# Split weights laid 2,080 bytes apart, at eight places modulo 64 bytes, in a three-block fp32 kernel

## The chip, the cores and the metric

The kernel runs on one core of one Trainium2 chip. The metric is the device time of one execution in microseconds. Before the change two runs took 833.51 and 834.58 us, median 834.05 us.

## What is computed

Three blocks follow each other on 4 sequences of 576 tokens with 512 features (2,304 tokens, 18 tiles of 128): a windowed attention with 8 heads, a block that mixes tokens and then features, and a feature block behind a normalization. Cut to what matters:

```python
def _moe_ref(x, w_tok1, w_tok2, w_ch1, w_ch2):
    h = np.maximum(x.transpose(0, 2, 1) @ w_tok1, 0.0) @ w_tok2
    u = x + h.transpose(0, 2, 1)
    return u + np.maximum(u @ w_ch1, 0.0) @ w_ch2          # 512 -> 1536 -> 512

def _moe2_ref(x, g_ln, w_ch1, w_ch2):
    mu, var = np.mean(x, -1, keepdims=True), np.var(x, -1, keepdims=True)
    xn = (x - mu) / np.sqrt(var + 1e-06) * g_ln
    return x + np.maximum(xn @ w_ch1, 0.0) @ w_ch2         # 512 -> 2048 -> 512

x = _attn_ref(q, k, v)        # window 128, a slope of distance for each head
return _moe2_ref(_moe_ref(x, ...), ...)
```

## The kernel before

**Split products.** A float32 product is made of three TensorE products. Each operand is split into a high part in float32r and a low part that holds the rest: a = ah + al, and a·b is taken as ah·bh + ah·bl + al·bh. Each product is one MATMUL, with a weight load (LDWEIGHTS) of its own for the operand that stands in the array. The other operand moves: 512 or 256 columns of 4 bytes are read from SBUF for each MATMUL.

**The two feature blocks.** They are walked in steps (list `steps`): a layer has three stages, of 8, 2 and 8 tiles of tokens, and each stage goes through all inner features, 12 blocks of 128 in layer 0 and 16 in layer 1. A step takes two blocks.

- `seven_products` (L1109) makes the first product of a wide step by Strassen-like sums: seven products of 6 MATMULs (L1125 to L1127). Here a split weight (w1h, w1l) stands in the array, 128 columns at a time, and a split input (x..., names xh and xl in the profile) moves, 512 columns.
- `two_blocks` (L1210) does a step of two tiles through `mm3` (L469 to L471): w1 stands, the inputs (fewh, fewl) move, 256 columns.
- `second` (L1223) makes the second product: inner features (hh, hl) stand, split weights (w2h, w2l) move, 512 columns (L1238 to L1240).
- `second_fast` (L1248) does the second product of one stage of layer 1 by seven products of 256 columns (L1275). There the moving weights are w2h and w2l in some products, and sums of weights in the buffers rw, rh and y in the others.

The first product of a step and the second product of the step before it are interleaved, six MATMULs of one by three to six of the other.

**Where the split weights come from.** `w_split` (L945) takes two buffers for each weight from the pool mlq: ACT copies the high part (L384), POOL or DVE subtracts the low part (L402, L400). `w2_of` (L1024) splits w2 only in the first stage of a layer; it stores both parts to DRAM, and in the later stages it loads them again into buffers of the same ring with two DMAs of 256 KB (L1038). The rings: w1h, w1l, w2h and w2l have four buffers each (W1_BUFS, W2_BUFS).

**Where buffers lie.** A `Buf` becomes a tile of a pool when it is first used (L101), and the tile framework lays a tag's buffers one behind another. A [128, 512] float32 buffer has 2,048 bytes in each partition. In the built program the pools stand so that each of the 16 split-weight buffers, each input buffer (pools mlp and mlr, and few in the pool hid) and each inner-feature buffer (hid) begins 32 bytes past a multiple of 64. The buffers rw, rh and y (pools raw and cvt) begin at a multiple of 64. The pool `even` (L359, 256 columns) takes up what lies between, so that mlp and mlr join without a gap. It is filled once with zeros by POOL (L777).

**What sets the order.** A list scheduler (`Plan.order`) gives every operation a place on its engine from fixed costs; addresses play no part in it. PE takes its MATMULs in that order.

Of the kernel before, what the change touches and what calls it, by code (L numbers as in the profile page):

```python
# [11 lines left out]
F32R = mybir.dt.float32r  # L12
# [12 lines left out]
P = 128  # L25
DM = H * D
# [8 lines left out]
CW = CT * P  # L35
HW = CW // 2
W_BUFS = 6
EVEN = 256
X_BUFS, TOK_RATE = 3, 3
Q_BUFS = 3  # L40
T_BUFS, PF_BUFS = 4, 4
W1_BUFS, W2_BUFS, ST_BUFS, H_BUFS = 4, 4, 6, 6
# [49 lines left out]
class Buf:  # L92


    def __init__(self, plan, pool, shape, dtype, tag, bufs):
        self.plan, self.pool, self.spec = plan, pool, (shape, dtype, tag, bufs)
        self.tile, self.ops, self.track = None, [], {}
        self.after, self.behind, self.first = [], None, set()

    @property  # L100
    def t(self):  # L101
        if self.tile is None:
            shape, dtype, tag, bufs = self.spec
            self.tile = self.plan.pools[self.pool].tile(shape, dtype, tag=tag, name=tag, bufs=bufs)
        return self.tile


class Part(Buf):


# [10 lines left out]
class Plan:  # L121
# [19 lines left out]

        self.chain = {}

    def buf(self, pool, shape, dtype, tag, bufs=1):
        b = Buf(self, pool, shape, dtype, tag, bufs)
        ring = self.rings.setdefault((pool, tag), [])
        if len(ring) >= bufs:
            b.after = [ring[-bufs]]
        if ring:
            b.behind = ring[-1]  # L150
        ring.append(b)
        return b
# [184 lines left out]
def block_kernel(tc, qT, kT, v, wt1, wt2, wa1, wa2, wb1, wb2, g, bias, out):  # L337
# [3 lines left out]
    buf = pl.buf  # L341

    def op(cost, emit, reads=(), writes=(), behind=()):
        return pl.op(cost, (lambda e: emit()) if len(cost) == 1 else emit, reads, writes, behind)
# [16 lines left out]


    even = buf("even", [P, EVEN], F32, "even")
    ident = buf("const", [P, P], F32, "ident")
    g_sb = buf("const", [P, DM // P, 1], F32, "g_sb")
    mv = buf("const", [P, NTILE, 2], F32, "mv")
    rstd = buf("const", [P, NTILE], F32, "rstd")
# [38 lines left out]
    def split(hi, ghi, lo, glo, x, gx, n, on_hi=("ACT", "DVE", "POOL"), on_lo=("DVE", "POOL")):  # L406
        copy(hi, ghi, x, gx, n, on_hi)
        minus(lo, glo, x, gx, hi, lambda: ghi().bitcast(F32), n, on_lo)
# [127 lines left out]
    def take_w():  # L536
        used[0] += 1
        return wtiles[used[0] - 1]
# [404 lines left out]
        return out  # L943

    def w_split(tag, bufs, x, get=None, n=DM, to=None):  # L945
        hi, lo = to or (buf("mlq", [P, DM], F32R, tag + p, bufs) for p in "hl")
        get = get or (lambda: x.t)
        split(hi, lambda: hi.t[:, :n], lo, lambda: lo.t[:, :n], x, get, n, ("ACT",))
        return hi, lo
# [12 lines left out]
    def w1_of(s, ahead=None):  # L962

        f1, f2 = take_w(), take_w()
        if len(steps[s][2]) == 2:
            out = [w_split("w1", W1_BUFS, x) for x in (f1, f2)]
            keep_taken(2)
            return out
# [23 lines left out]
        def parts(early=lambda: None):  # L992
            w0 = w_split("w1", W1_BUFS, f1, to=early())
            if ahead != "few":
                sums_a()
            w1 = w_split("w1", W1_BUFS, a, all_of(a), to=early())
            if ahead != "few":
                sums_b()
            return w0, w1
# [18 lines left out]
    parts2, sums2 = {}, {}  # L1018

    def fast2(s):  # L1020
        layer, c, _, n = steps[s]
        return (layer, c) in FAST2 and n < (NF1, NF2)[layer] // 2 - 1

    def w2_of(s):  # L1024
        out = []
        layer, c, _, n = steps[s]
        last = [mark[0]]
        for f in (2 * n, 2 * n + 1):
            if c == 0:
                x = w_split("w2", W2_BUFS, take_w())  # L1030
                for p, y in zip("hl", x):
                    d = parts2[layer, f, p] = buf("dram", [P, DM], F32, f"d2{layer}{f}{p}")
                    op({"DMA": 728}, lambda d=d, y=y: nc.sync.dma_start(out=d.t, in_=y.t.bitcast(F32)), [y], [d], last)
            else:
                x = []
                for p in "hl":
                    y, d = buf("mlq", [P, DM], F32R, "w2" + p, W2_BUFS), parts2[layer, f, p]
                    op({"DMA": 728}, lambda d=d, y=y: nc.sync.dma_start(out=y.t.bitcast(F32), in_=d.t), [d], [y])  # L1038
                    x.append(y)
            out.append(x)  # L1040
        if c == 0 and (layer, 2) in FAST2 and n < (NF1, NF2)[layer] // 2 - 1:
            keep_sums(layer, n, wtiles[used[0] - 2:used[0]], last)
        return sums_of(layer, n, out) if fast2(s) else out

    def keep_sums(layer, n, w, last):

        x0, x1 = w
        places = few()
        d = {p: buf("dram", [P, 2 * DM], F32, f"ds{layer}{n}{p}") for p in "hl"}

        def all_of(k):
            return places[0], lambda: places[0].t.bitcast(F32)[:, k, :DM]

        def part(c):
            return (places[0], c // 2), lambda: places[0].t.bitcast(F32)[:, c // 2, c % 2 * HW:(c % 2 + 1) * HW]

        def half(x, c):
            return x, lambda: x.t[:, c * HW:(c + 1) * HW]

        def sub(c, a, b):  # L1060
            (x, k), get = part(c)
            minus((x, c), get, *a, *b, HW, ("POOL",))

        def at(c):
            return (places[0], c), part(c)[1]

        sub(0, half(x0, 1), half(x0, 0))
        sub(1, half(x1, 1), at(0))
        sub(2, half(x0, 1), half(x1, 1))
        sub(3, half(x1, 0), at(1))  # L1070
        for k in range(2):
            f, h = [(places[0], 2 * k), (places[0], 2 * k + 1)], (places[1], k)

            def gf(k=k):
                return places[0].t[:, k, :DM]

            def gh(k=k):
                return places[1].t[:, k, :DM]

            copy(h, gh, f, lambda gf=gf: gf().bitcast(F32), DM, ("ACT",))  # L1080
            minus(f, gf, f, lambda gf=gf: gf().bitcast(F32), h, lambda gh=gh: gh().bitcast(F32), DM, ("POOL",))
            for p, z, gz in (("h", [h], gh), ("l", f, gf)):
                op({"DMA": 728}, lambda k=k, p=p, gz=gz: nc.sync.dma_start(
                    out=d[p].t[:, k * DM:(k + 1) * DM], in_=gz().bitcast(F32)), z, [(d[p], k)], last)
        sums2[layer, n] = d

    def sums_of(layer, n, parts):

        d = sums2[layer, n]
        hi = buf("raw", [P, 2 * DM], F32R, "rw", 2)  # L1090
        hs = [((hi, None), lambda k=k: hi.t[:, k * HW:(k + 1) * HW]) for k in range(4)]
        if n % 2:
            lo = [buf("cvt", [P, DM], F32R, "y", 2) for _ in range(2)]
            ls = [((lo[k // 2], None), lambda k=k: lo[k // 2].t[:, k % 2 * HW:(k % 2 + 1) * HW]) for k in range(4)]
        else:
            lo = [buf("raw", [P, 2 * DM], F32R, "rh", 1)]
            ls = [((lo[0], None), lambda k=k: lo[0].t[:, k * HW:(k + 1) * HW]) for k in range(4)]
        for p, xs in (("h", [hi]), ("l", lo)):
            w = 2 * DM // len(xs)
            for k, x in enumerate(xs):  # L1100
                op({"DMA": 1456 / len(xs)}, lambda p=p, k=k, x=x, w=w: nc.sync.dma_start(
                    out=x.t.bitcast(F32), in_=d[p].t[:, k * w:(k + 1) * w]), [d[p]], [x])
        w = {f"t{k + 1}": (hs[k], ls[k]) for k in range(4)}
        for j, x in enumerate(parts):
            for c in range(2):
                w[f"{j}{c}"] = tuple(((y, None), lambda y=y, c=c: y.t[:, c * HW:(c + 1) * HW]) for y in x)
        return w
# [278 lines left out]
    for s in range(len(steps) + 1):  # L1386
# [5 lines left out]
        layer, c, tiles, n = steps[s]  # L1392
# [37 lines left out]
        if s + 1 < len(steps):  # L1430
            w1 = begun() if begun else w1_of(s + 1)
        w2 = w2_of(s)
        pl.shift = STAGE_SHIFT
        stage_w(STAGE_RATES.get((layer, c), 0))
# [46 lines left out]
```

## Time and profile before

| | |
|---|---|
| median of 2 runs | 834.05 us (833.51 to 834.58) |
| the profiled execution | 835.71 us, of which the span from first to last instruction is 834.0 us |
| PE busy | 820.6 us, 98% of the span |
| share of PE in the chain that ended last | 90% |
| granted TensorE clock | 1.00 (2.4 GHz) in all of the span |
| DMA | 179.20 MB, mean 215 GB/s |

The rows below come from this profiled execution. A MATMUL's row shows a start and a modelled duration. The MATMULs are pipelined and their durations overlap, so what one of them costs is the spacing, from its start to the start of the next. The view of the chain in order of time shows such spacings: its pieces stand end to end.

### The profile page before, as it was taken

The numbers are of one execution on the slowest core, as the hardware profiler recorded it, in microseconds if no ns is written. First come the engines' busy times: TensorE is split into PE (matmuls) and PEld (weight loads), VectorE is DVE, ScalarE is ACT, GpSimd is POOL, SyncE is SP. The second block draws the span as 40 slices with busy tenths as digits, with TensorE's granted clock in tenths as the row PEclk, the third lists the DMA queues.
The fourth block names the chain that finished last, engine by engine and source line by source line (L and its number), as shares of the span: only waits on it lengthen the run. The fifth ranks groups of instructions, "written<-read, shape, count | busy, mean of one in ns | idle before, by whom it ended". The sixth has DMA issues, their size and how long they took to land.

```text
span 834.0 us, 14315 instructions
## 1 busy us (share of the span) xinstructions
PE 820.6 (98%) x4732; PEld 691.7 (83%) x4732; DVE 658.4 (79%) x1372; ACT 430.8 (52%) x1015; POOL 466.4 (56%) x708
## 2 busy tenths in 40 slices
PE   8998999999999999999999999999999999999998
PEld 6777788888888898888888888888889889999996
DVE  5786878978898989978889868989666767777785
ACT  6887777633344535234368333447456634444440
POOL 2685366755454667543338666857533656666650
PEclk9999999999999999999999999999999999999999
DMA  8679657443678799977861544888977663443202
GB/s 301 194 215 275 227 173 224 134 158 111 232 252 283 272 335 334 348 266 266 269 238 55 186 158 137 296 306 299 356 250 243 219 226 136 131 141 122 103 26 101
DMA packets 79898, 179.20 MB, mean 215 GB/s; under 512 B 9040, under 2 KB 9168, under 8 KB 79824
## 3 DMA queue, kind: packets, MB, share of 16 engines
q1 hardware_dynamic: 79344, 176.98, 63.3%
q0 software_dynamic: 480, 1.31, 0.6%
q8 instruction: 37, 0.61, 0.3%
q14 instruction: 37, 0.30, 0.1%
HBM read 138.15 MB, written 38.80 MB: 212 GB/s over the span
## 4 chain that ended last, share of the span: by engine, by line
PE 90%; DVE 3%; DMA 3%; ACT 1%; POOL 1%; issue 1%; SPq 0%; ACTq 0%; DVEq 0%; POOLq 0%
PE tok L1238 11%; PE tok L1240 11%; PE tok L1239 10%; PE b L1125 10%; PE b L1126 10%; PE b L1127 10%; PE tok L1275 5%; PE p L1275 4%; PE ps_v L637 3%; PE ps_s L625 2%; PE p L878 2%; PE b L471 2%; PE b L470 2%; PE b L469 2%; PE tok L766 1%; PE tok L764 1%
## 5 line engine op out<-in xcount | busy, mean ns | idle before, releaser
L1243 DVE TENSOR_TENSOR u<-tok,u 128x512 f32<-128x512 f32 x196 | 133.8, 685 | 47.8 <-PE tok L1240 46.1
L1238 PE MATMUL tok<-w2h,hh 128*128 128x512 f32 x392 | 154.2, 393 | 0.2 <-DVE u L1243 0.2
L1240 PE MATMUL tok<-w2h,hl 128*128 128x512 f32 x392 | 153.0, 390 | 0.2 <-DVE hl L958 0.2
L1239 PE MATMUL tok<-w2l,hh 128*128 128x512 f32 x392 | 152.9, 390 | 0.0
L1125 PE MATMUL b<-xh,w1h 128*128 128x512 f32 x384 | 150.4, 392 | 0.0
L1126 PE MATMUL b<-xl,w1h 128*128 128x512 f32 x384 | 149.8, 390 | 0.0
L1127 PE MATMUL b<-xh,w1l 128*128 128x512 f32 x384 | 149.5, 389 | 0.0
L402 POOL TENSOR_TENSOR w1l<-w,w1h 128x256 fp32r<-128x256 f32 (+1 forms) x110 | 77.4, 725 | 103.5 <-ACT w1h L384 99.0
L956 ACT ACTIVATE hh<-b 128x512 fp32r<-128x512 f32 (+1 forms) x112 | 58.7, 542 | 147.1 <-PE b L1127 104.1
L958 DVE SCALAR_TENSOR_TENSOR hl<-b,hh 128x512 fp32r<-128x512 f32 (+1 forms) x112 | 67.4, 617 | 26.3 <-ACT hh L956 25.7
L1240 PEld LDWEIGHTS tok<-w2h,hl 128*128 128x128 f32 x392 | 73.6, 188 | 16.4 <-DVE hl L958 0.8
L1238 PEld LDWEIGHTS tok<-w2h,hh 128*128 128x128 f32 x392 | 73.7, 188 | 15.5 <-DVE u L1243 1.3
L402 POOL TENSOR_TENSOR w1l<-st,w1h 128x256 fp32r<-128x256 f32 x70 | 55.3, 811 | 55.5 <-ACT w1h L384 49.7
L1239 PEld LDWEIGHTS tok<-w2l,hh 128*128 128x128 f32 x392 | 73.7, 188 | 14.3
L1127 PEld LDWEIGHTS b<-xh,w1l 128*128 128x128 f32 x384 | 72.1, 188 | 15.4
L1125 PEld LDWEIGHTS b<-xh,w1h 128*128 128x128 f32 x384 | 72.3, 188 | 13.9 <-DVE b L400 0.2
L1126 PEld LDWEIGHTS b<-xl,w1h 128*128 128x128 f32 x384 | 72.2, 188 | 13.5
L445 ACT ACTIVATE e<-rh 128x512 bf16<-128x512 bf16 (+2 forms) x65 | 41.5, 639 | 62.1 <-DMA rh<-wb 35.6
L675 ACT ACTIVATE pr<-t,mn 128x128 f32<-128x128 f32 x144 | 55.9, 392 | 13.7 <-DVE mn L666 13.7
L692 POOL TENSOR_SCALAR_AFFINE_SELECT pf<-pf 128x512 f32<-128x512 f32 x64 | 42.5, 663 | 30.1 <-ACT pf L384 27.9
L400 DVE TENSOR_TENSOR b<-b,p 128x512 f32<-128x512 f32 x56 | 38.9, 694 | 19.8 <-PE b L1127 18.7
L402 POOL TENSOR_TENSOR st<-w 128x128 f32<-128x128 f32 x68 | 37.3, 573 | 24.1 <-PE tok L1240 5.5
(188 smaller groups left out, 1909.7 us busy)
## 6 DMA issues: line engine op xcount, KB each, us to landing
w<-d SPq DMA_DIRECT2D x86, 256.0 KB, 4.1
rw<-wb SPq DMA_DIRECT2D x32, 512.0 KB, 5.3
rh<-wb SPq DMA_DIRECT2D x32, 512.0 KB, 5.3
rw<-wa SPq DMA_DIRECT2D x24, 512.0 KB, 4.5
rh<-wa SPq DMA_DIRECT2D x24, 512.0 KB, 4.4
d<-y SPq DMA_DIRECT2D x30, 256.0 KB, 5.0
keys<-kT SPq DMA_DIRECT2D x18, 256.0 KB, 4.3
q<-qT SPq DMA_DIRECT2D x18, 256.0 KB, 4.5
```

Source lines behind the costliest of these rows:

```text
L402: ENGINE[e].tensor_tensor(get()[:, c], ga()[:, c], gb()[:, c], alu)
L675: op({"ACT": 580}, lambda m=m: nc.scalar.activation(out=pr.t[:, m], in_=t.t[:, m], func=AF.Exp, bias=mn.t[:, m:m + 1], scale=-1.0, accum_o ...
L956: op({"ACT": act(n, True)}, lambda: nc.scalar.activation(out=hh.t[:, c], in_=go(), func=AF.Relu), [o], [(hh, key)])
L958: mark[0] = op({"DVE": dve(n)}, lambda: nc.vector.scalar_tensor_tensor(out=hl.t[:, c], in0=go(), scalar=0.0, in1=hh.t[:, c].bitcast(F32), ...
L1125: nc.tensor.matmul(g.t, wh.t[:, w], xh.t, start=start and k == 0, stop=False, skip_group_check=True)
L1126: nc.tensor.matmul(g.t, wh.t[:, w], xl.t, start=False, stop=False, skip_group_check=True)
L1127: nc.tensor.matmul(g.t, wl.t[:, w], xh.t, start=False, stop=stop and k == 1, skip_group_check=True)
L1238: nc.tensor.matmul(o.t, hh.t[:, c:c + P], wh.t, start=j == 0, stop=False)
L1239: nc.tensor.matmul(o.t, hh.t[:, c:c + P], wl.t, start=False, stop=False)
L1240: nc.tensor.matmul(o.t, hl.t[:, c:c + P], wh.t, start=False, stop=j == 1)
L1243: op({"DVE": dve(DM)}, lambda o=o, i=i: nc.vector.tensor_tensor(u[i].t, o.t, u[i].t, ALU.add), [o], [u[i]])
L1275: nc.tensor.matmul(o.t[:, p], x()[:, c], y(), start=start and p == 0 and k == 0, stop=stop and p == 1 and k == 2, skip_group_check=True)
```

## The change

The split-weight buffers get 8 more columns (`EXTRA`), so that they lie 2,080 bytes apart. A new class `Place` lets the data begin at a column of its own in each buffer of the ring, from `FIRST`: columns 0, 0, 4, 4 for the high parts and 2, 2, 6, 6 for the low ones. In the changed program the four buffers of w1h (and of w2h) begin 32, 0, 48 and 16 bytes past a multiple of 64, those of w1l (and w2l) 40, 8, 56 and 24. The inputs and the inner features still begin 32 bytes past a multiple of 64. The 16 longer buffers take 512 bytes more; the pool `even` shrinks by as much, from 256 to 128 columns, and mlp and mlr move up by 512 bytes. The instructions and their order are the same on every engine, but for the width of the fill of `even`.

```diff
-EVEN = 256
+EVEN, EXTRA = 128, 8
+FIRST = {"h": (0, 0, 4, 4), "l": (2, 2, 6, 6)}
...
+class Place(Buf):
+    def __init__(self, plan, pool, n, dtype, tag, bufs, first):
+        super().__init__(plan, pool, [P, n + EXTRA], dtype, tag, bufs)
+        self.cols = slice(first, first + n)
+
+    @property
+    def t(self):
+        return super().t[:, self.cols]
...
-    def buf(self, pool, shape, dtype, tag, bufs=1):
-        b = Buf(self, pool, shape, dtype, tag, bufs)
+    def buf(self, pool, shape, dtype, tag, bufs=1, places=None):
         ring = self.rings.setdefault((pool, tag), [])
+        if places:
+            b = Place(self, pool, shape[1], dtype, tag, bufs, places[len(ring) % bufs])
+        else:
+            b = Buf(self, pool, shape, dtype, tag, bufs)
...
-        hi, lo = to or (buf("mlq", [P, DM], F32R, tag + p, bufs) for p in "hl")
+        hi, lo = to or (buf("mlq", [P, DM], F32R, tag + p, bufs, FIRST[p]) for p in "hl")
...
-                    y, d = buf("mlq", [P, DM], F32R, "w2" + p, W2_BUFS), parts2[layer, f, p]
+                    y, d = buf("mlq", [P, DM], F32R, "w2" + p, W2_BUFS, FIRST[p]), parts2[layer, f, p]
```

## Rows read from the trace of the kernel before

**Rows 1.** The page: busy time, and the granted clock in 40 slices.

```profile
PE 820.6 (98%) x4732; PEld 691.7 (83%) x4732; DVE 658.4 (79%) x1372; ACT 430.8 (52%) x1015; POOL 466.4 (56%) x708
...
PEclk9999999999999999999999999999999999999999
```

**Rows 2.** The page: the chain that ended last, by engine.

```profile
PE 90%; DVE 3%; DMA 3%; ACT 1%; POOL 1%; issue 1%; SPq 0%; ACTq 0%; DVEq 0%; POOLq 0%
```

**Rows 3.** Groups by line and shape, 512 columns: busy us, mean ns, idle before.

```profile
L1238 PE MATMUL tok<-w2h,hh 128*128 128x512 f32 x392 | 154.2, 393 | 0.2 <-DVE u L1243 0.2
L1240 PE MATMUL tok<-w2h,hl 128*128 128x512 f32 x392 | 153.0, 390 | 0.2 <-DVE hl L958 0.2
L1239 PE MATMUL tok<-w2l,hh 128*128 128x512 f32 x392 | 152.9, 390 | 0.0
L1125 PE MATMUL b<-xh,w1h 128*128 128x512 f32 x384 | 150.4, 392 | 0.0
L1126 PE MATMUL b<-xl,w1h 128*128 128x512 f32 x384 | 149.8, 390 | 0.0
L1127 PE MATMUL b<-xh,w1l 128*128 128x512 f32 x384 | 149.5, 389 | 0.0
```

**Rows 4.** Tile w1h: its MATMULs, duration ns min/median/max.

```profile
L1126 PE MATMUL b<-xl,w1h x384: 387/389/402, 168.8 to 818.8; 128*128 128x512 f32 x192
L470 PE MATMUL b<-fewl,w1h x112: 279/283/287, 284.5 to 660.4; 128*128 128x256 f32 x112
```

**Rows 5.** The chain in order of time, 456 to 460 us: start us, us, what.

```profile
456.13 0.23 PE tok L1240
...
457.72 0.23 PE b L1125
...
459.53 0.23 PE tok L1240
```

**Rows 6.** The same view, 690 to 701 us, in the stage of `second_fast`.

```profile
689.95 0.72 PE tok L1275 x6
690.67 0.23 PE b L1125
...
691.83 0.23 PE b L1127
...
693.42 0.70 PE p L1275 x6
694.12 0.70 PE tok L1275 x6
694.82 0.23 PE b L1125
...
695.98 0.23 PE b L1127
```

**Rows 7.** Groups by line and shape, 256 columns.

```profile
L1275 PE MATMUL tok<-w2l,hh 128*128 128x256 f32 x84 | 23.8, 283 | 0.0
L1275 PE MATMUL p<-rw,hl 128*128 128x256 f32 x56 | 15.7, 280 | 0.0
```

**Rows 8.** Stretches with many loads of w2: busy us by engine, clock, DMA share, GB/s.

```profile
290.00:316.00 26.00, 26.00 (x167) 23.63 (x166) 21.52 (x48) 10.20 (x22) 16.62 (x21) 1.00 0.96 338
316.00:340.00 24.00, 24.00 (x118) 20.05 (x117) 23.65 (x44) 10.92 (x20) 18.87 (x30) 1.00 0.96 339
```

**Rows 9.** DMA issues from 316 to 340 us: first and last of the 12 w2 loads to 2011l.

```profile
w2h<-d206h SPq DMA_DIRECT2D x1, 256.0 KB, 2.9
...
w2l<-d2011l SPq DMA_DIRECT2D x1, 256.0 KB, 6.6
```

## The prediction

> **What bounds the kernel now.** I read the page first: PE is busy for 98% of the span, and the granted clock is full, 2.4 GHz, in every slice [rows 1]. The chain that ended last is 90% PE [rows 2]. So neither a wait nor the clock is left to gain much from; what counts is how far apart PE's MATMULs start. Six groups of 512 columns carry the two feature blocks, 3 x 392 + 3 x 384 = 2,328 MATMULs [rows 3], and the change touches one operand of each: w1 stands in L1125 to L1127, w2 moves in L1238 to L1240.
>
> What one costs is its spacing. From 456.13 to 459.53 us the chain has 15 steps without a break, 3.40 us, so 226.7 ns each [rows 5]; 512 columns at 2.4 GHz are 213.3 ns, so 13 ns of each are something else. In the same way six MATMULs of 256 columns with w2 moving take 0.72 us, 120.0 ns each [rows 6], against 106.7 ns: again 13 ns. The extra does not grow with the columns; it comes once for a MATMUL, as its weight load does.
>
> Two things in the rows say that addresses and history matter for it. First, the buffers rw, rh and y begin at a multiple of 64 bytes and w2 begins 32 past one; both move in L1275, against inner features that begin 32 past one. With w2 moving six take 0.72 us, with the sums moving 0.70 us, so 120.0 and 116.7 ns [rows 6]; the modelled durations differ alike, 283 and 280 ns [rows 7]. Second, spacing settles. Behind a run of 256 columns the first MATMULs of 512 are dearer: from 690.67 to 691.83 us five take 1.16 us, 232 ns each, and from 694.82 to 695.98 us again five in 1.16 us; from 691.83 to 693.42 us seven take 1.59 us, 227 ns each [rows 6]. So the read of the moving operand and the load of the next weights seem to fall into a step with each other, and where all operands begin at the same place of 64 bytes that step is held. I read it so: 227 ns is the settled spacing, 232 ns the unsettled one.
>
> The settled duration is 389 ns, the median of L1126 [rows 4]; it stands for 227 ns of spacing, so a duration is 162 ns longer than its spacing. The four groups that do not open a product have means of 390, 390, 390 and 389 ns [rows 3], 389.75 together, or 227.75 of spacing. With 227 and 232 as the two kinds, (227.75 - 227) / 5 is 15% unsettled today.
>
> **The change, part by part.** *Instructions:* none is added, removed or moved, on any engine or queue; the fill of `even` gets narrower, once, at the start, where PE isn't waiting for it. Cost 0. PE's waits stay; at the change of pools near 150 us a few writes of ACT, DVE and POOL wait for other loads of the attention, landed long before. Cost 0.
>
> *First products (3 x 384 MATMULs of 512 columns).* The moving inputs stay at 32; the weights that stand alternate h, h, l within a product, and l begins 8 bytes past h. So from one MATMUL to the next the two reads stand to each other in a new way, and the step that is held today is broken at every third one. *Second products (3 x 392).* The inner features stay; the moving w2 alternates l and h and then goes to the pair of the other block: new places again. After an interruption it takes about five MATMULs to settle [rows 6]; the places now change more often than that. So I take four fifths as unsettled: 0.8 x 232 + 0.2 x 227 = 231.0 ns, against 227.75 today, +3.25 ns each. For 2,328 that is +7.6 us. Bounds: from -0.75 ns (all settle) to +4.25 ns (none does), -1.7 to +9.9 us. No row shows a MATMUL whose place changes each time; the nearest rows are the unsettled ones, and I stand near them.
>
> *Gain from unequal places.* A moving operand at 0 instead of 32 saves 3.3 ns settled [rows 6]. The changed w2 stands at all eight places, at distances of 0, 8, 16, 24 and 32 bytes from the inner features; if the gain grows evenly with distance, its mean is half, 1.7 ns. I count it where the moving operand is what changes, as in those rows: 3 x 392 of 512 columns and 3 x 84 in L1275 [rows 3, 7], 1,428 x 1.7 = -2.4 us. Bounds: 0, and the full 3.3 ns on these and on all first products too, also the 3 x 112 of 256 columns in two-tile steps (x112, [rows 4]): 2,328 + 252 + 336 = 2,916 x 3.3 = -9.6 us.
>
> The Trainium skill, in "SBUF — State Buffer", Door 1 (the note on cachelines), says that SBUF is read in lines of 16 bytes and that each new line costs. The low parts now begin 8 past a multiple of 16, so a read of 2,048 bytes would touch 129 lines and not 128. A line of four elements is 1.7 ns at 2.4 GHz, and a third of 2,916 MATMULs would pay it: by that page 1.6 us more than my sum. No row of this kernel has such a start, so I leave it to the range.
>
> *Writers and DMAs.* ACT, POOL and DVE write the split parts at the new places, and 256 KB loads land at them. Every tile in this trace begins at 0 or 32 modulo 64, so no row shows their price. At no extra cost they stay hidden: the chain has 3% DMA and 1% ACT and POOL each [rows 2]. Their bound is the last rival's price. I take 0.
>
> **Sum.** +7.6 - 2.4 = +5.2 us. On the profiled execution (span 834.0 us plus 1.7 around it, 835.7) that gives 840.9 us; this execution lies 1.7 us over the median of the runs, 834.05, so for the median I predict 839 us (+0.6%).
>
> **Rivals.**
>
> *It gains: unequal places part the two reads.* For it speaks the one comparison the trace has, 116.7 against 120.0 ns [rows 6]. Against it: that pair differs in the pool too, and it was settled on both sides. Worked out: -9.6 us on all 2,916, and -1.7 us if all settle as well: 834 - 11.3 = 823 us, 1.4% faster. Over 2% needs 5.8 ns on each of 2,916, nearly half of the 13 ns, and no row shows more than 3.3.
>
> *The places mean nothing.* Then 120.0 against 116.7 would come from the pool or from what ran before, and spacing stays: 834 us. Against it: both kinds of six stand next to each other in one stage, with one kind of stationary operand [rows 6]. This is the result that the Trainium skill gives: "TensorE: Matmul & The Clock Gate", Part 2, says that PE has two independent read ports and that loading the next weights takes nothing from the moving read. The 13 ns and the 3.3 ns of this trace agree badly with that, so I hold it for less likely than the forecast.
>
> *Nothing settles, and the worst steps become common.* The step at the start of an unsettled run takes more than its mean: two MATMULs of the five reach 236 ns if the other three are at 229, as 1.16 us allow. Place: each pair h, l in both products. If every one of 2,328 went to 236 ns, 8.25 ns more, that is +19 us: 853 us, 2.3% slower. It decides from the point where the mean spacing passes 235 ns. Against it: the rows never stay there for more than a few.
>
> *Loads to new places are slower.* From 316 to 340 us the DMA engines are 96% busy at 339 GB/s, and so from 290 to 316 us [rows 8]. In 24 us they move 8.1 MB, of which the 12 loads from d206h to d2011l [rows 9] are 3.1 MB, 38%. If such a load took twice its engine time, the stretch would need 38% more: 9.1 us; with as many loads before 316 us some 9 us again. Total 834 + 18 = 852 us. It needs a price for the start of a row of 2,048 bytes that is as large as the row, and PE to wait at once: today the loads take 2.9 to 6.6 us to land and PE isn't held by them.
>
> **How the numbers follow.** Chances: forecast (a loss of 0.1 to 1.3%) 0.50; gain by unequal places 0.18; nothing changes 0.14; worst steps common 0.12; slow loads 0.06. The range is 822 to 855 us: below it is a gain larger than the one comparison shows, above it two mishaps together; about 1 in 10 lies outside. The likeliest case alone has 835 to 845 us. 2% of the time before, 16.7 us, is about what a measurement of this kernel can tell from no change. Faster by more needs the rival of unequal places to do more than its row: 0.05. Slower by more comes from the last two, about half of each, and a little from the forecast's tail: 0.12. The rest, 0.83, is within 2%.
>
> **What would show it.** Right: means of L1126, L1127, L1239 and L1240 rise from 390 to about 393 ns, the chain's steps of 512 columns take 0.23 with a mean near 231 ns and no stretch stays at 226.7 ns; L1275 with w2 moving falls below 283 ns. Wrong: means below 389 ns (the gain), means unchanged at 390 (no effect of places), or rows in which PE waits for a load of w2 between 290 and 340 us (slow loads). If the 512-column MATMULs settle again in each product, at some other spacing than 227, the step "four fifths unsettled" is the one that failed.

## The result, and the profile after

The changed kernel takes 844.19 us (median of 2 runs, 843.72 to 844.66) against 834.05 us before: ratio 1.0122, 95% interval 1.0078 to 1.0165. It is slower by 1.2%, less than 2%. The span of the profiled execution grew from 834.0 to 842.9 us.

The page of the changed kernel, busy time, granted clock and chain (they answer to [rows 1, 2]; lines of code are 16 higher):

```profile
PE 830.2 (98%) x4732; PEld 693.0 (82%) x4732; DVE 660.8 (78%) x1372; ACT 430.4 (51%) x1015; POOL 465.8 (55%) x708
...
PEclk9999999999999999999999999999999999999999
...
PE 93%; ACT 2%; DVE 2%; DMA 1%; POOL 1%; issue 0%; ACTq 0%; POOLq 0%; DVEq 0%
```

PE is busy 9.6 us longer with the same 4,732 MATMULs at the same clock; DVE, ACT and POOL keep their times within 2.4 us. The chain holds still more PE. So no wait came in: PE itself became slower.

The groups of 512 columns, by line and shape (to be read beside [rows 3]; mean ns is the last number before the second bar):

```profile
L1254 PE MATMUL tok<-w2h,hh 128*128 128x512 f32 x392 | 155.0, 395 | 0.0
L1256 PE MATMUL tok<-w2h,hl 128*128 128x512 f32 x392 | 154.9, 395 | 0.5 <-DVE hl L974 0.5
L1255 PE MATMUL tok<-w2l,hh 128*128 128x512 f32 x392 | 153.9, 393 | 0.0
L1141 PE MATMUL b<-xh,w1h 128*128 128x512 f32 x384 | 151.9, 396 | 0.0
L1142 PE MATMUL b<-xl,w1h 128*128 128x512 f32 x384 | 150.9, 393 | 0.0
L1143 PE MATMUL b<-xh,w1l 128*128 128x512 f32 x384 | 150.8, 393 | 0.0
```

Every group's mean rose, by 2 to 5 ns. Group by group, rise times count: 392 x (2 + 5 + 3) + 384 x (4 + 3 + 4) ns = 3.9 + 4.2 = 8.1 us. That is nearly all of the 8.9 us by which the span grew. The loss is spread about evenly over both products.

The tile w1h (to [rows 4]): the median of L1142 went from 389 to 392 ns, while the 256-column one fell from 283 to 280:

```profile
L1142 PE MATMUL b<-xl,w1h x384: 389/392/399, 170.2 to 827.5; 128*128 128x512 f32 x192
L486 PE MATMUL b<-fewl,w1h x112: 276/280/287, 287.9 to 668.5; 128*128 128x256 f32 x112
```

Durations are modelled; starts are the surer sign. The first products of one step stand together near the end of a stage: 24 MATMULs with 23 spacings and no break, the same 24 in every kernel here. Timeline of PE, start us and duration us, first and last of the 24, before and after:

```profile
567.04 0.39 PE L1125 MATMUL b<-xh,w1h 128*128 128x512 f32 x1
...
572.26 0.39 PE L1127 MATMUL b<-xh,w1l 128*128 128x512 f32 x1
```

```profile
575.08 0.40 PE L1141 MATMUL b<-xh,w1h 128*128 128x512 f32 x1
...
580.42 0.40 PE L1143 MATMUL b<-xh,w1l 128*128 128x512 f32 x1
```

Before, 5.22 us / 23 = 227.0 ns; after, 5.34 / 23 = 232.2 ns. It does not come back to 227 within the run. Over the whole program the starts show the same: the longest row of spacings of 225 to 227 ns, among the MATMULs of 512 columns of both products, has 343 of them before and three after.

No row lays the loss on the loads of w2. From 316 to 340 us, where the DMA engines are fullest (to [rows 8, 9]; the same views of the changed kernel):

```profile
316.00:340.00 24.00, 24.00 (x124) 20.14 (x123) 23.39 (x42) 13.28 (x24) 17.59 (x26) 1.00 0.97 347
```

```profile
w2h<-d206h SPq DMA_DIRECT2D x1, 256.0 KB, 4.4
...
w2l<-d2011l SPq DMA_DIRECT2D x1, 256.0 KB, 5.9
```

They land in 4.4 to 6.0 us at new places, 2.9 to 6.6 before, and PE is busy in all of the 24 us.

### The profile page after: what moved, and what is told of

It reads as the page before. It is cut to its first block, busy times and chain, and to the rows that moved or that the text cites. A ratio compares the mean times of both kernels' runs of the same rounds, so it can differ in the third digit from the quotient of the medians.

```text
span 842.9 us, 14316 instructions
## 1 busy us (share of the span) xinstructions
PE 830.2 (98%) x4732; PEld 693.0 (82%) x4732; DVE 660.8 (78%) x1372; ACT 430.4 (51%) x1015; POOL 465.8 (55%) x708
## 4 chain that ended last, share of the span: by engine, by line
PE 93%; ACT 2%; DVE 2%; DMA 1%; POOL 1%; issue 0%; ACTq 0%; POOLq 0%; DVEq 0%
PE tok L1256 11%; PE tok L1254 11%; PE b L1141 11%; PE tok L1255 11%; PE b L1143 11%; PE b L1142 11%; PE tok L1291 5%; PE p L1291 4%; PE ps_s L641 3%; PE ps_v L653 3%; PE p L894 2%; PE b L485 2%; PE b L486 2%; PE b L487 2%; ACT pr L691 1%; PE ps_t L698 1%
## 5 line engine op out<-in xcount | busy, mean ns | idle before, releaser
L1256 PE MATMUL tok<-w2h,hl 128*128 128x512 f32 x392 | 154.9, 395 | 0.5 <-DVE hl L974 0.5
L1142 PE MATMUL b<-xl,w1h 128*128 128x512 f32 x384 | 150.9, 393 | 0.0
L1142 PEld LDWEIGHTS b<-xl,w1h 128*128 128x128 f32 x384 | 72.1, 188 | 14.8
```

Source lines behind the costliest of these rows:

```text
L1142: nc.tensor.matmul(g.t, wh.t[:, w], xl.t, start=False, stop=False, skip_group_check=True)
L1256: nc.tensor.matmul(o.t, hl.t[:, c:c + P], wh.t, start=False, stop=j == 1)
```

## The experiments

Of each run I give the mean of the spacing from start to start, taken from the trace over all MATMULs of 512 columns, without those in which PE waited. "First" is the product with w1, "second" that with w2. In the kernel before all these operands lie at the same place modulo 512 bytes (the places are those of the built programs; the traces hold no addresses). Each ratio is taken against runs of the kernel before that were made beside that run; their medians go from 834.05 to 836.22 us.

| run | first | second | time us, median | ratio (95%) |
|---|---|---|---|---|
| before | 227.7 | 227.7 | 834.05 | |
| the change | 231.3 | 231.5 | 844.19 | 1.0122 (1.0078 to 1.0165) |
| u0 | 231.6 | 232.0 | 843.09 | 1.0077 (1.0049 to 1.0105) |
| u8 | 232.8 | 233.1 | 846.10 | 1.0117 (1.0084 to 1.0151) |
| u4 | 231.7 | 231.9 | 845.41 | 1.0108 (1.0079 to 1.0136) |
| u2 | 232.3 | 233.9 | 846.11 | 1.0114 (1.0086 to 1.0143) |
| x512 | 227.7 | 227.6 | 835.83 | 1.0010 (0.9997 to 1.0024) |
| x64 | 230.8 | 230.5 | 842.81 | 1.0088 (1.0066 to 1.0110) |
| x32 | 233.5 | 229.3 | 842.80 | 1.0090 (1.0058 to 1.0123) |
| wx32 | 228.4 | 232.8 | 841.63 | 1.0078 (1.0046 to 1.0110) |
| r128 | 232.6 | 232.8 | 847.75 | 1.0152 (1.0093 to 1.0211) |
| r480 | 233.4 | 229.1 | 844.82 | 1.0116 (1.0087 to 1.0146) |
| r448 | 232.5 | 233.4 | 845.98 | 1.0130 (1.0086 to 1.0175) |
| w1only | 231.3 | 229.1 | 839.61 | 1.0052 (1.0031 to 1.0072) |

**Is it the place modulo 64?** My theory was the prediction's: the kernel before holds a step because all operands have one place, and alternating places break it. The rivals: distance itself costs; reads that begin off a multiple of 16 bytes cost (the "line theory"); the move of the pools costs. Four kernels put all split weights at one place modulo 64, high and low parts alike. To have room for any column they make the buffers 16 columns longer and drop `even`:

```diff
-EVEN, EXTRA = 128, 8
-FIRST = {"h": (0, 0, 4, 4), "l": (2, 2, 6, 6)}
+EXTRA = 16
+FIRST = {"h": (c,) * 4, "l": (c,) * 4}      # c = 0, 8, 4, 2 in u0, u8, u4, u2
-    open_pool("even", side="right")
-    even = buf("even", [P, EVEN], F32, "even")
-        op({"POOL": 100}, lambda: nc.gpsimd.memset(even.t, 0.0), [], [even])
```

Expected of u0 (all back at 32 modulo 64):

> All split weights back at 32 past a multiple of 64, but in longer buffers (2,112 bytes apart) and with the pool `even` gone, so that inputs lie 1,024 bytes further up than before. Settling theory (a new place from one MATMUL to the next costs): settles as before, mean spacing of the 512-column MATMULs of both products 227 to 228 ns, time 832 to 836 us. Layout theory (the move of the pools and the longer distance between buffers cost, not the places): stays near 844 us with a mean near 231 ns.

Expected of u8 (all at 0):

> As u0, but all 16 split-weight buffers at 0 modulo 64, 32 from inputs and inner features, the same for high and low parts. Settling theory: one place for all, so it settles; spacing near 227 ns or, as with 256 columns, down to 223 ns: 824 to 836 us. Distance theory (any place unequal to the other operand's costs): 840 us or more, mean near 231 ns. Gain theory of the blind rivals: 823 to 827 us.

Expected of u4 (all at 48):

> As u0, but all split weights at 48 modulo 64, 16 from the other operands. Settling theory: settles, 227 ns or less, 824 to 836 us. Distance theory: 838 us or more. Line theory (only starts that are no multiple of 16 cost): 834 us.

Expected of u2 (all at 40):

> As u0, but all split weights at 40 modulo 64, 8 from the other operands and no multiple of 16. Settling theory: settles, 227 to 229 ns, 830 to 838 us. Line theory: a line more in each read, at least 1.7 ns on each of 2,916 MATMULs, 5 us over u0, and as much over u4. Distance theory: 838 us or more.

By their spacings all four lose as much as the change, u0 too, where every place modulo 64 is that of before. (By the ratio u0 loses 0.8% and the change 1.2%; the intervals overlap.) Groups of u0:

```profile
L1252 PE MATMUL tok<-w2l,hh 128*128 128x512 f32 x392 | 154.8, 395 | 0.0
...
L1139 PE MATMUL b<-xl,w1h 128*128 128x512 f32 x384 | 151.3, 394 | 0.0
```

So modulo 64 is the wrong measure, and my theory fell in the form that I had given it: u8, u4 and u2 do not alternate within a product and lose too. The distance theory missed u0. u2, off a multiple of 16, is 0.7 us over u4 and 3.0 over u0, not 5; but the three differ in their distances as well, so whether such a start has a price of its own stays open. What u0 left was the layout: inputs 1,024 bytes up, or buffers 2,112 bytes apart, which puts neighbours at different places modulo 128 and more.

**Place of the inputs alone.** The next runs start from the kernel before, with 2,048 bytes between buffers. Only `even` shrinks, which lifts the inputs (in pools on the right side), or unused bytes ahead of the ring lift the weights too:

```diff
-EVEN = 256
+EVEN = 128                    # x512; 240 in x64; 248 in x32 and wx32
...
                 open_pool(n, reuse_waits="tile", **kw)
+                if n == "mlq":                                                # wx32 alone
+                    pl.pools[n].tile([P, 8], F32, tag="fill", name="fill")
```

Expected of x512, x64, x32 and wx32, in this order:

> The kernel before with only the pool `even` at 128 columns: inputs (mlp, mlr) lie 512 bytes higher, as in the changed kernel; split weights stay 2,048 bytes apart at their old places. If the move of the inputs by 512 bytes costs by itself (relation modulo 2,048): first products near 231 ns, second products 227.7 ns, 838 us. If what counts is the relation modulo 512 or less: as before, 227.7 ns in both, 834 us.

> The kernel before with `even` at 240 columns: inputs 64 bytes higher, so that they stand to the weights as before modulo 64 and 64 off modulo 128. If only the place modulo 64 counts: 227.7 ns in both products, 834 us. If the relation of the two operands counts modulo more than 64 (up to 512), first products rise to 230 ns or more and second products stay: 837 us or more. If only a change from one MATMUL to the next costs (the relation is the same in all first products here): 227 to 229 ns, 834 to 836 us.

> The kernel before with `even` at 248 columns: inputs 32 bytes higher, at 0 modulo 64, weights at 32, as the sums of weights and the inner features stand to each other in L1275. If that relation is good with 512 columns as it is with 256, first products settle at 223 to 224 ns: 830 us. If equal places are what settles: first products 230 ns or more, second products 227.7 ns: 837 us or more.

> Split weights and inputs both 32 bytes higher (32 unused bytes ahead of the ring, `even` at 248 columns), inner features stay: first products have equal places, all at 0 modulo 64; in second products w2 moves at 0 and the inner features stand at 32. If equal places settle: first products 227.7 ns, second products 230 ns or more, 837 us or more. If the pair (0, 32) is good: second products 223 to 224 ns, 830 us. If 0 modulo 64 is itself good for a moving operand: both near 224 ns, 826 us.

x512 takes the time of the kernel before: the move of the inputs that is part of the change costs nothing. x64 loses 8 us though every operand stays at 32 modulo 64: the places count modulo more than 64. x32 and wx32 part the two products. In x32 first products are unequal (233.5 ns) and second ones equal (229.3); in wx32 it is the other way (228.4 and 232.8), with the equal pair at 0 modulo 64. So, with 512 columns, no place is good or bad in itself; what counts is that the moving operand and the standing one have the same. The timeline of the same 24 first products, x64, then x32, then wx32:

```profile
570.72 0.40 PE L1125 MATMUL b<-xh,w1h 128*128 128x512 f32 x1
...
576.00 0.39 PE L1127 MATMUL b<-xh,w1l 128*128 128x512 f32 x1
```

```profile
572.45 0.40 PE L1125 MATMUL b<-xh,w1h 128*128 128x512 f32 x1
...
577.82 0.40 PE L1127 MATMUL b<-xh,w1l 128*128 128x512 f32 x1
```

```profile
573.26 0.39 PE L1125 MATMUL b<-xh,w1h 128*128 128x512 f32 x1
...
578.48 0.40 PE L1127 MATMUL b<-xh,w1l 128*128 128x512 f32 x1
```

5.28, 5.37 and 5.22 us for 23 spacings: 229.6, 233.5 and 227.0 ns, against 227.0 before. In x32 the spacings repeat nearly in fours (about 234, 234, 231, 235 ns), so it does settle, but at a dearer spacing. That is against my reading of "unsettled": an unequal pair has a settled spacing of its own.

The second products of x32 and x64, whose operands are equal, were expected to stay at 227.7 ns and did not: x32 has 229.3, and x64 has 230.5, nearly what its unequal first products have (230.8). What they lose is the passage from an unequal product, as the end of x64 shows, where 48 second products follow each other. The chain in order of time, the first of them, the eighth and the last but one:

```profile
824.02 0.24 PE tok L1238
...
825.65 0.23 PE tok L1239
...
834.49 0.23 PE tok L1239
```

The first seven spacings take 1.63 us, 232.9 ns each; the other 39 take 8.84 us, 226.7 ns each. Elsewhere the two products alternate every few MATMULs, and the equal one seldom settles.

The durations can mislead: x64's L1126 has a mean of 391 ns, as x512's has, though its starts lie 3 ns further apart.

**Modulo what?** Three more pairs, with the ring and the inputs lifted by amounts of their own:

```diff
+EVEN = 192                    # r128: inputs +256 bytes; 72 in r480: +736; 32 in r448: +896
+                    pl.pools[n].tile([P, 32], F32, tag="fill", name="fill")   # weights +128; +256; +448
```

Expected of r128, r480 and r448, in this order:

> Weights 128 bytes past the inner features, inputs 128 bytes past the weights (modulo 512), all buffers 2,048 bytes apart and at 32 modulo 64. If the relation of the two operands counts modulo 128: settles at 226.7 ns in both products, 834 us. If it counts modulo 256 or 512: both products above 228 ns, 838 to 846 us. If any fixed relation would settle at the same spacing (theory of a step broken by alternation): 227 to 228 ns, 834 us.

> Weights 256 bytes past the inner features, inputs 32 bytes below the weights (480 modulo 512). If the relation counts modulo 256: second products 227.7 ns; if modulo 512: above 228 ns. First products: if the sign of the distance does not matter, near 233 ns as with inputs 32 bytes above; if it does, another settled spacing, which may lie under 226.7 ns.

> Weights 64 bytes below the inner features, inputs 64 bytes below the weights (448 modulo 512): w2 as the moving operand stands to the next weights as inputs do. If the sign does not matter: a cycle near 229 ns in both products as with inputs 64 above, 838 us. If equal places are the only good ones: above 228 ns in both. A cheaper relation than equal places would show as a run of spacings under 226 ns and a time under 833 us.

r128 loses in both products (modulo 128 is refuted). r480's second products, 256 bytes off, have a mean of 229.1 ns, as the equal ones of x32 have, and settle where no other product comes between. The program ends with 48 second products; the starts of the first 47 give 46 spacings, in r480, then in wx32, where w2 is 32 bytes off:

```profile
828.52 0.40 PE L1238 MATMUL tok<-w2h,hh 128*128 128x512 f32 x1
...
838.95 0.39 PE L1239 MATMUL tok<-w2l,hh 128*128 128x512 f32 x1
```

```profile
824.96 0.39 PE L1238 MATMUL tok<-w2h,hh 128*128 128x512 f32 x1
...
835.69 0.39 PE L1239 MATMUL tok<-w2l,hh 128*128 128x512 f32 x1
```

10.43 / 46 = 226.7 ns against 10.73 / 46 = 233.3 ns. So equal modulo 256 bytes is equal. For the 24 first products of r448 (64 bytes below) the starts give:

```profile
577.53 0.39 PE L1125 MATMUL b<-xh,w1h 128*128 128x512 f32 x1
...
582.89 0.39 PE L1127 MATMUL b<-xh,w1l 128*128 128x512 f32 x1
```

5.36 / 23 = 233.0 ns, while 64 bytes above had 229.6: the sign matters. Of 0, 32, 64, 128, 256, 448 and 480 bytes only 0 and 256 reach a mean of 226.7 ns, and none goes below. No run beats the kernel before.

**The change for w1 alone.** With the changed kernel's buffers for w1, the old ones for w2, and all but w1 equal modulo 256:

```diff
-EVEN, EXTRA = 128, 8
+EVEN, EXTRA = 192, 8
-        hi, lo = to or (buf("mlq", [P, DM], F32R, tag + p, bufs, FIRST[p]) for p in "hl")
+        hi, lo = to or (buf("mlq", [P, DM], F32R, tag + p, bufs, FIRST[p] if tag == "w1" else None) for p in "hl")
-                    y, d = buf("mlq", [P, DM], F32R, "w2" + p, W2_BUFS, FIRST[p]), parts2[layer, f, p]
+                    y, d = buf("mlq", [P, DM], F32R, "w2" + p, W2_BUFS), parts2[layer, f, p]
```

Expected:

> The changed kernel with the longer buffers and the eight places for w1 alone; w2 lies 2,048 bytes apart again and it, the inputs and the inner features are equal modulo 256. If what costs is the place of the two operands to each other modulo 256: first products stay near 231.3 ns as in the changed kernel, second products, whose operands are equal, come back to 227.7 to 229.3 ns with half or more at 226 or 227 (what they lose is the passage from an unequal product before), 838 to 841 us. If what costs is the alternation of places in PE's stream as a whole, second products stay above 230 ns, 843 us. If w2's places or its loads carried the loss, first products fall to 228 ns too, 835 us.

Measured 839.61 us, with the spacings that the first theory asks for: 231.3 ns in first products, 229.1 in second ones. The first 47 of the 48 second products at the end:

```profile
821.90 0.40 PE L1254 MATMUL tok<-w2h,hh 128*128 128x512 f32 x1
...
832.37 0.39 PE L1255 MATMUL tok<-w2l,hh 128*128 128x512 f32 x1
```

10.47 / 46 = 227.6 ns, with the passage at its start; from the ninth on every spacing is 226 or 227. By the table, 1,152 x 3.6 + 1,176 x 1.4 ns = 5.8 us are lost; the ratio gives 4.3 us (2.6 to 6.0). The change costs through both operands, each in its own product.

## Why the prediction was right, and where its steps were not

*The forecast* was 839 us, slower by 0.6%; it is slower by 1.2%, near the upper end of the 0.1 to 1.3% that the forecast allowed. What bounds the kernel was read rightly: the loss lies in the spacing of PE's MATMULs, not in a wait or a load. The mechanism behind the size was read wrongly, and that the size came out is in good part luck.

*Step "four fifths unsettled", +7.6 us.* Its size was about right: the four groups that don't open a product have a mean of 393.5 ns instead of 389.75, so 231.5 ns of spacing, where I had worked out 231.0; 3.75 ns on 2,328 are 8.7 us (8.3 us by the starts of the two profiled executions). Its reason was not. I took the alternation of places for the cause. The runs show that any pair not equal modulo 256 loses the 227 ns, however constant (x32, x64, r128, r448). Unequal pairs settle at means of 229.0 to 233.4 ns; that 232 ns, read off MATMULs behind an interruption, lies among them is luck. In the changed kernel, counted modulo 256 and against the other operand, the four high buffers lie at 0, 32, 80 and 112 bytes and the four low ones at 136, 168, 216 and 248: one of eight is equal. The 2,080 bytes between buffers are enough for that, whatever `FIRST` says; u0, with 2,112 bytes and one place modulo 64, shows the same loss. What the alternation adds to it was not tried by itself. The signs named in the prediction came true (means of 393, 393, 393 and 395 ns, no stretch at 226.7 ns, L1275 with w2 moving below 283 ns), but unequal pairs give the same signs, so they did not test the reason.

*Step "gain from unequal places", -2.4 us.* This term failed. I took a pair of 256 columns, 116.7 against 120.0 ns [rows 6], and laid it on MATMULs of 512 columns. There the same distance of 32 bytes costs 6.5 ns (x32, 233.5 against 227.0) instead of saving 3.3. The reading itself holds for 256 columns, and wx32 tests it, where w2 is moved by 32 bytes and the inner features stay: w2's MATMULs in L1275 have a median spacing of 117 ns, where before has 120, and their durations fall from 283 to 280 ns:

```profile
L1275 PE MATMUL tok<-w2l,hh 128*128 128x256 f32 x84 | 23.5, 280 | 0.0
```

In the changed kernel the gain with 256 columns is 0.5 us in the two-tile steps and 0.1 us in L1275, by the starts.

*Why +5.2 us became +10.1.* By the starts of the two profiled executions, the 512-column MATMULs of both products took 8.3 us more; the term for them was +7.6. The 256-column MATMULs with split weights took 0.6 us less, which is all that there is of the -2.4. All that the change does not touch took 1.2 us more; that rest is 1.4 us shorter in x512's trace than in that of before, so it differs as much from one execution to another. Together that is 8.9 us. The last 1.2 us come from the medians: the profiled execution of before lay 1.7 us over its median, that of after 0.5.

*Rivals.* "The places mean nothing" and "unequal places gain" are refuted, for 512 columns, by x32 and wx32. "Loads to new places are slower" shows in no row. "Worst steps common" asked for 236 ns throughout: the highest mean of any run is 233.9 (u2).

The Trainium skill, in "TensorE: Matmul & The Clock Gate", Part 2, has the load of the next weights take nothing from the moving read. These runs fit badly with that: moving one operand by 32 bytes against the other, with nothing else changed, takes the spacing from 227.0 to 233.5 ns (x32). Whether the two reads meet in SBUF or elsewhere, no run here tells, nor why 13 ns stay with equal places.

## What to carry to other kernels

When a kernel is bound by back-to-back MATMULs with a weight load each, the place of the two operands against each other is worth up to 3% of their time here, with 512 columns (226.7 against 233.3 ns). With 256 columns equal places are not the cheapest, so the two widths have to be weighed against each other. Read it off the starts in a run without breaks, not off the durations or the busy share. Padding a ring of buffers moves every buffer against the other operand; where the operands were equal modulo 256 bytes, a distance that is a multiple of 256 keeps them so.

## What was not expected of the hardware

- The modulus is 256 bytes, not 64: 64 bytes and 128 bytes off cost 2.6 and 6.5 ns with 512 columns (x64, r128), 256 bytes off nothing (r480).
- An unequal pair settles too, in a pattern of its own to be seen in the trace's starts: constant 233.3 ns at 448 bytes, 235 and 232 ns in turn at 480, 229 and 237 in turn at 128. The means of these three and of 32 bytes agree within 0.2 ns (233.3 to 233.5); only 64 bytes lies between, with 226, 229 and 232 ns in turn.
- With 256 columns the order is another: in r448, with w2 64 bytes below the inner features, w2's MATMULs in L1275 have a median spacing of 114 ns, 120 before, and L1275 with w2l moving a mean duration of 277 ns, 283 before.

The group of r448 for that last point:

```profile
L1275 PE MATMUL tok<-w2l,hh 128*128 128x256 f32 x84 | 23.3, 277 | 0.0
```
